# One GELU for both blocks in group 0, w1's last rows loaded whole, powers on GpSimd and a new order in a state-space and MLP kernel

## The chip, the cores and the metric

The kernel runs on one core of a Trainium2 chip. The core has a matrix engine (TensorE, PE in the profile), an engine for element-wise work (VectorE, DVE), one for activation functions (ScalarE, ACT), a general one (GpSimd, POOL), a queue engine that mostly starts transfers (SyncE, SP), and 16 DMA engines. Each engine takes its own instructions strictly in order, and they wait for one another through semaphores. The metric is the device time of one execution in microseconds; smaller is better.

## The reference

The input x has 2048 rows (a sequence) of 448 channels, in bf16. A layer norm gives xn. One path is a diagonal complex state-space layer: with dt = exp(log_dt) and a complex Lambda, each state decays by exp(dt * Lambda) from row to row, takes B_bar @ xn and is read by C. The other path is an MLP over a second layer norm: 448 to 1792 channels, GELU, back to 448. Its silu gates the first path.

```python
def _A_ref(x, ...):
    Lam, Bmat, Cmat = Lambda_re + 1j * Lambda_im, B_re + 1j * B_im, C_re + 1j * C_im
    dt = jnp.exp(log_dt)
    Lam_bar = jnp.exp(dt * Lam)
    B_bar = ((Lam_bar - 1.0) / Lam)[:, None] * Bmat
    Bu = jnp.einsum("bld,pd->blp", x + 0j, B_bar)
    for t in range(L):
        h = Lam_bar[None, :] * h + Bu[:, t, :]
    y = 2.0 * jnp.einsum("blp,dp->bld", hseq, Cmat).real + x * Dskip
def _B_ref(x, w1, b1, w2, b2):
    h = _gelu(_layernorm(x) @ w1 + b1)
    return h @ w2 + b2
xn = _layernorm(x)
return x + _A_ref(xn, ...) * _silu(_B_ref(xn, ...))
```

## The kernel before, in words

**Tiling.** The 2048 rows form four groups g of 512. A group has two blocks b; a block has 128 partitions, each with two neighbouring rows (par 0 and 1). The MLP's hidden width is 14 tiles of 128, worked in seven pairs.

**Stages of a group.** `ln_stats`, `ln_scale` and `ln_apply` give xn and xn2 (the norm of the norm, folded into one scaling). `ln_scale` takes an inverse square root, on POOL with the operation power (L480) or on DVE by Newton steps (L478 to L488). DMA transposes give xnT and xn2T. `mm1_run` multiplies xn2T by w1 (PE at L801) and applies GELU out of PSUM (ACT at L805) into gT. `mm2` multiplies by w2 (PE at L828), adds b2 (DVE at L831), and the silu follows. `bu` (L729) is the input product of the state-space layer, `ssm` (L744 to L775) its scan on DVE, `m0` (L697, L712) products of CQ and Bn that are needed once, and `ym` (L871 to L877) the output product. The final multiply and add stand at L885 to L891, and the add runs on DVE or POOL. `combine` (L658 to L661) scales rows of B and C into Bn, CQ and CZ: one scaled copy into `tmp` (ACT or DVE) and one fused multiply-add on DVE.

**mm1.** Each matmul uses 64 of the 128 partitions, so two run side by side on the halves of the array. A pair of tiles takes a first phase of 6 and a second of 8 matmuls, into two PSUM banks out of the list `MB`; `pairs` says which bank pair a tile pair takes. The 448 rows of w1 lie in four slots: 0 to 2 hold rows 0 to 383, and slot 3 holds rows 320 to 447. Its low half (rows 320 to 383) is a copy of the high half of slot 2, made by DVE or ACT at L352; its high half is loaded. w1 is loaded in four column chunks, each as a large piece (`w1_c`) and a small one (`w1r_c`).

**Group 0.** It starts while its data arrive. Block 0 is normalised first (`first_stats`, `first_apply`): ACT forms the inverse root as exp(-0.5 ln v) at L434/L435 for block 0 and L438/L439 for block 1. PE transposes the blocks at L460 instead of a DMA. mm1 of group 0 then has five pairs for block 0 alone, two pairs for both blocks, and five pairs for block 1 alone. A one-block pair has matmuls and GELUs of 256 columns, a two-block pair of 512. dt and the size of the pole are exponentials on ACT, at L533 and L541. After those ACT loads the GELU's table (L443), and it changes tables twice more near group 0 (L614 for silu, L618 for GELU).

**What sets the order.** A `Plan` records every task with what it reads and writes. `link` derives the dependencies, and `emit` issues the tasks in the fixed list `ORDER` and puts semaphore waits where they are needed. A task recorded with `either` has two engines to choose from, and the list `SECOND` names those that take the second. Thus each engine's queue, and the queues of transfers on SP and POOL, are a projection of this one list. SP's queue starts with x, w1, more of x, w2, then B and C, and then the transposes.

## Time and profile before

| what | value |
|---|---|
| median of 3 runs | 153.23 us (153.21 to 153.32) |
| profiled execution | span 151.8 us |
| PE busy | 147.1 us (97%) |
| DVE busy | 127.6 us (84%) |
| ACT busy | 99.0 us (65%) |
| POOL busy | 42.1 us (28%) |
| moved by DMA | 14.73 MB, mean 97 GB/s |

The span is the profiled execution from its first to its last event; the runs' times are those of whole executions and hold some work around it. An engine's share is its busy time over the span; register, branch and semaphore instructions are not counted. The page also cuts the span into 40 slices. A group line gives source line, engine, operation, tiles, shape and count, then busy time with the mean of one in ns, then the idle time just before and what ended it. A row of the timeline gives its start and length in us, and `x42` says that 42 like instructions stand in it. An issue line of the DMA view gives the size and the time from issue to landing.

### The profile page before, as it was taken

What the parts mean: (1) busy time and instruction counts of PE and PEld (TensorE: products, weight loads), DVE (VectorE), ACT (ScalarE), POOL (GpSimd) and SP (SyncE); (2) the same over time, 40 slices, a digit from 0 to 9 for tenths busy, and PEclk for the clock granted to TensorE, in tenths of its full rate; (3) what the DMA queues carried; (4) which work ended last, traced back from release to release, by engine and by line L of the source; (5) the groups of instructions that cost most, each with busy time, mean ns of one, the idle gap of its engine ahead of it and who ended that gap; (6) DMA issues with size and microseconds to landing.
All of it is one profiled execution on the core that took longest, in us unless ns stands there. A gap on an engine that the chain in (4) does not pass through costs nothing.

```text
span 151.8 us, 2974 instructions
## 1 busy us (share of the span) xinstructions
PE 147.1 (97%) x1127; PEld 86.6 (57%) x1127; DVE 127.6 (84%) x267; ACT 99.0 (65%) x183; POOL 42.1 (28%) x101
## 2 busy tenths in 40 slices
PE   7899999999999999999999999999999999999992
PEld 7785755454566577545444556764454666555551
DVE  2874999999978979999999996379968726999984
ACT  3888996988789559997898610463579834067400
POOL 5376827153020920010456006200072031000201
PEclk9999999999999999999999999999999999999999
DMA  4999999989997300700003032610331001100022
GB/s 116 262 305 390 266 202 138 219 152 133 165 261 180 65 0 0 138 0 4 0 0 63 4 60 45 154 60 4 60 101 23 0 4 57 64 0 0 4 84 98
DMA packets 31236, 14.73 MB, mean 97 GB/s; under 512 B 24752, under 2 KB 30774, under 8 KB 31222
## 3 DMA queue, kind: packets, MB, share of 16 engines
q1 hardware_dynamic: 30912, 14.26, 41.8%
q0 software_dynamic: 160, 0.23, 1.0%
q8 instruction: 9, 0.15, 0.4%
q10 hardware_dynamic: 150, 0.05, 0.1%
q14 instruction: 5, 0.04, 0.1%
HBM read 6.89 MB, written 1.84 MB: 57 GB/s over the span
## 4 chain that ended last, share of the span: by engine, by line
PE 80%; DVE 9%; DMA 4%; SPq 4%; issue 2%
PE psum L828 23%; PE psum L801 22%; PE psum L729 14%; PE psum L871 13%; DMA x_all<-in_A_x_dram 4%; PE psum L874 4%; SPq L84 4%; PE psum L712 3%; DVE xn_sb L499 2%; DVE lnst L399 1%; DVE s_w L628 1%; PE psum L877 1%; DVE o L831 1%; PE psum L697 1%; DVE tmp L891 1%
## 5 line engine op out<-in xcount | busy, mean ns | idle before, releaser
L801 PE MATMUL psum<-xn2T,w_sb 64*128 64x512 bf16 (+1 forms) x462 | 44.6, 345 | 0.3 <-ACT xn2T L417 0.2
L828 PE MATMUL psum<-w_sb,gT 128*128 128x448 bf16 x224 | 44.5, 353 | 0.2 <-DVE o L831 0.2
L805 ACT ACTIVATE gT<-psum,b1f 128x512 bf16<-128x512 f32 (+1 forms) x66 | 35.9, 625 | 10.4 <-PE psum L801 10.2
L801 PEld LDWEIGHTS psum<-xn2T,w_sb 64*128 64x128 bf16 x462 | 24.1, 109 | 19.8 <-ACT gT L805 2.3
L828 PEld LDWEIGHTS psum<-w_sb,gT 128*128 128x128 bf16 x224 | 21.5, 98 | 20.7 <-DVE o L831 0.6
L417 ACT ACTIVATE u_sb<-psum 128x512 bf16<-128x512 f32 (+2 forms) x22 | 10.5, 478 | 23.0 <-PE psum L729 22.7
L729 PE MATMUL psum<-xnT,BT 128*128 128x256 bf16 x196 | 24.0, 273 | 0.0
L729 PEld LDWEIGHTS psum<-xnT,BT 128*128 128x128 bf16 x196 | 18.9, 98 | 5.4 <-issue 1.1
L891 POOL TENSOR_TENSOR tmp<-t,x_all 128x448 bf16<-128x448 bf16 x5 | 5.2, 1032 | 33.1 <-DVE t L888 30.7
L753 DVE TENSOR_TENSOR_SCAN s_w<-dk,vs 128x774 f32<-128x774 f32 x8 | 14.0, 1760 | 0.1
L500 ACT ACTIVATE xn_sb<-x_all,lnw 128x448 bf16<-128x448 bf16 (+2 forms) x21 | 13.0, 662 | 1.2 <-DVE xn_sb L499 1.1
L417 ACT ACTIVATE vs<-s_w 64x256 bf16<-64x256 f32 (+2 forms) x16 | 10.9, 681 | 2.6 <-DVE s_w L753 1.5
L871 PE MATMUL psum<-CZ,h_sb 128*128 128x448 bf16 x56 | 11.9, 352 | 0.0
L871 PE MATMUL psum<-CQ,h_sb 128*128 128x448 bf16 (+2 forms) x54 | 10.5, 332 | 0.0
L399 DVE BATCH_NORM_STATS2 lnst<-x_all 128x6 f32<-128x448 bf16 x12 | 7.1, 617 | 3.4 <-DMA x_all<-in_A_x_dram 3.4
L831 DVE TENSOR_TENSOR o<-psum,b2bc 128x448 f32<-128x448 f32 x16 | 9.7, 614 | 0.2
L871 PEld LDWEIGHTS psum<-CZ,h_sb 128*128 128x128 bf16 x56 | 5.4, 98 | 4.7 <-DVE lnmv L405 0.4
L871 PEld LDWEIGHTS psum<-CQ,h_sb 128*128 128x128 bf16 x54 | 5.1, 98 | 4.0 <-DVE t L885 0.4
L874 PE MATMUL psum<-M,xnT 128*128 128x448 bf16 x32 | 7.4, 352 | 0.0
L480 POOL TENSOR_TENSOR lnw<-lnw,mhalf 128x8 f32<-128x8 f32 x3 | 7.2, 2404 | 0.3
L883 DVE TENSOR_TENSOR Cr<-psum,xd 128x448 f32<-128x448 f32 x7 | 4.3, 620 | 3.5 <-PE psum L877 3.4
L499 DVE TENSOR_SCALAR xn_sb<-x_all,lnw 128x448 bf16<-128x448 bf16 (+2 forms) x19 | 6.9, 396 | 0.0
(160 smaller groups left out, 189.1 us busy)
## 6 DMA issues: line engine op xcount, KB each, us to landing
out_dram<-tmp SPq DMA_DIRECT2D x7, 224.0 KB, 2.0
x_all<-in_A_x_dram SPq DMA_DIRECT2D x3, 448.0 KB, 4.0
w_sb<-in_B_w_dram SPq DMA_DIRECT2D x3, 448.0 KB, 8.4
w_sb<-in_B_w_dram SPq DMA_DIRECT2D x3, 384.0 KB, 4.8
vs<-in_A_C_re_dram SPq DMA_DIRECT2D x1, 392.0 KB, 11.6
Bn<-in_A_B_im_dram SPq DMA_DIRECT2D x1, 336.0 KB, 10.2
Bn<-in_A_B_re_dram SPq DMA_DIRECT2D x1, 336.0 KB, 10.5
vs<-in_A_C_im_dram SPq DMA_DIRECT2D x1, 336.0 KB, 10.8
```

The source lines that it names most:

```text
L399: dve([lambda e, b=b, par=par, q=q: e.bn_stats(lnst[:, q, :], x_all[:, 2 * g + b, par, :])], [f"x{2 * g + b}"] , [f"st{q}"], 0.62, prio)
L417: kb.either(("act", [lambda e, o=o, i=i: e.activation(o, i, ACT.Copy) for o, i in pairs]), ("dve", [lambda e, o=o, i=i: e.tensor_copy(o, i ...
L499: on = [("dve", [lambda e, o=o, i=i: e.tensor_scalar(o, i, rs, nb, op0=ALU.mult, op1=ALU.add) for o, i in parts], 0.4, 0.12), ("act", [lam ...
L500: ("act", [lambda e, o=o, i=i: e.activation(o, i, ACT.Identity, bias=nb, scale=rs) for o, i in parts], 0.75, 0.2)]
L729: fns = [lambda e, r=r, m=m, d=d: e.matmul(psum[:, 4, r * NK:(r + 1) * NK], BT[:, m, d, :], xnT[:, gx, d, :], start=(d == 0), stop=(d == 6 ...
L753: dve(lambda e, so=so, vi=vi: e.tensor_tensor_scan(so, dk[:].rearrange("p i c -> p (i c)"), vi, 0.0, ALU.mult, ALU.add), ["v", "vl", "dk", ...
L801: return lambda e: e.matmul(view(bk[k]), w1_sb[rows, d, fcol(2 * j + k)], rhs[rows, d, :, :], start=not second and n == 0, stop=second and ...
L805: act([lambda e, k=k: e.activation(gT[:, gb, 2 * j + k, :].rearrange("p (r c) -> p r c", r=2)[:, :, cols], view(bk[k]), ACT.Gelu_apprx_tan ...
L828: fns = [lambda e, fi=fi: e.matmul(psum[:, bk, 0:D], gT[:, gb, fi, q * 128:(q + 1) * 128], w2_sb[:, fi, :], start=(fi == 0), stop=(fi == N ...
L831: dve(lambda e: e.tensor_tensor(o2[:, fb, :], psum[:, bk, 0:D], b2bc[:], ALU.add), [f"ps{bk}", "b2bc"], [f"oo{fb}"], 0.62, prio - 76)
L871: fns = [lambda e, k=k: e.matmul(psum[:, bk, c0:c1], h_sb[:, hb, k, k0:k0 + 128], cm[:, k, c0:c1], start=(k == 0), stop=False) for k in ra ...
L874: fns += [lambda e, d=d: e.matmul(psum[:, bk, c0:c1], xnT[:, gx, d, xs], M0[:, d, c0:c1], start=False, stop=(d == 3)) for d in range(4)]
```

## The change

The change has five parts.

1. w1's slot 3 is loaded whole (128 rows of each chunk, from row 320 on), and the four copies at L352 are gone.
2. Block 1's inverse root is formed by one small DVE operation and a power on POOL, in place of Ln and Exp on ACT.
3. dt and the pole's size are formed by POOL as powers of e; a new tile `euler` holds e. The load of the GELU's table does not wait for them or for block 1's root.
4. mm1 of group 0 runs pairs 1, 2, 0 for block 0 without a GELU, the same pairs for block 1 in the same banks, then a GELU over both blocks for each of the three; pairs 3 to 6 run for both blocks at once.
5. `ORDER` and `SECOND` are new throughout. w2's first piece is issued ahead of the last w1 piece and of x for group 1, and C_im ahead of w2's last piece; both row broadcasts by POOL (b2 and Dskip) are issued together; the first product `m0` follows the first `bu` of group 0; five of the final adds go from DVE to POOL.

```diff
--- before.py
+++ after.py
@@ -160,27 +160,26 @@
 ORDER = [int(k) for k in """
-0 13 19 47 9 16 18 20 14 1 94 26 17 95 91 27 92 21 15 24 48 4 96 12 108 93 90 109 97 104 103 25 105 99 22 98 49 50 55 5 51 65 106 2 110 100 111 107 29
+17 9 16 20 14 0 91 92 19 25 18 88 4 44 15 13 1 21 89 93 87 106 45 90 46 5 107 2 96 102 24 27 101 26 3 22 108 48 100 23 12 103 29 104 30 47 28 94 52
...
 SECOND = [int(k) for k in """
-45 53 54 61 63 66 69 74 76 83 112 130 133 158 160 162 163 165 177 184 185 187 189 190 220 222 224 226 228 230 238 248 249 258 266 268 331 362 364 365
+42 50 51 54 59 69 72 73 74 75 76 81 83 84 98 105 110 119 144 151 152 185 209 211 213 217 219 223 225 229 235 237 247 251 257 325 334 339 341 343 351
...
@@ -223,6 +222,7 @@
 
         ident = SB("ident", [128, 128])
         mhalf = SB("mhalf", [128, 1, 1], F32)
+        euler = SB("euler", [128, 1], F32)
         dk = SB("dk", [128, 3, NK + 2], F32)
         iota = dk[:, 0, 0:NK]
         sgn = SB("sgn", [128, 4], F32)
@@ -324,6 +324,7 @@
             pool(lambda e: e.memset(M0[:, 3, :], 0.0), [], ["M0p"], 0.3, S0 + 1)
             pool(lambda e: e.memset(h_sb[:, :, :, 0:2], 0.0), [], ["hp0", "hp1"], 0.2, S0 + 1)
             pool(lambda e: e.memset(mhalf[:], -0.5), [], ["mhalf"], 0.1, S0 + 1)
+            pool(lambda e: e.memset(euler[:], math.e), [], ["euler"])
             pool(lambda e: e.memset(eps[:, 0:1], LN_EPS), [], ["eps"], 0.1, S0)
             pool(lambda e: e.memset(eps[:, 1:2], LN_EPS * LN_EPS), ["eps"], ["eps"], 0.1, S0)
 
@@ -345,11 +346,7 @@
             def ldw1(cs, prio):
                 a, w = CH[cs[0]][0] * 128, sum(CH[c][1] for c in cs) * 128
                 ld("sp", w1_sb[:, 0:3, a:a + w], dram_ap(B_w1, a, [[F, 128], [128 * F, 3], [1, w]]), [f"w1_{c}" for c in cs], 384 * w * 2, prio, dur=0.55)
-                ld("sp", w1_sb[64:128, 3, a:a + w], dram_ap(B_w1, 384 * F + a, [[F, 64], [1, w]]), [f"w1r_{c}" for c in cs], 64 * w * 2, prio)
-                for c in cs:
-                    a, w = CH[c][0] * 128, CH[c][1] * 128
-                    low, high = w1_sb[0:64, 3, a:a + w], w1_sb[64:128, 2, a:a + w]
-                    kb.either(("dve", lambda e, low=low, high=high: e.tensor_copy(low, high)), ("act", lambda e, low=low, high=high: e.activation(low, high, ACT.Copy)), [f"w1_{c}"], [f"w1c_{c}"])
+                ld("sp", w1_sb[:, 3, a:a + w], dram_ap(B_w1, 320 * F + a, [[F, 128], [1, w]]), [f"w1r_{c}" for c in cs], 128 * w * 2, prio)
 
             LW = ((0,), (1,), (2,), (3,))
 
@@ -434,13 +431,13 @@
                         kb.add("act", [lambda e, var=var, r1=r1: e.activation(r1, var, ACT.Ln, scale=1.0 + LN_EPS, bias=eps[:, 1:2]),
                                        lambda e, r1=r1: e.activation(r1, r1, ACT.Exp, scale=-0.5)], [f"mv0_{q}", "eps", "warm"], [f"r1{q}"], chain=True)
                     elif par == 1:
-                        vs2, rs2 = lnmv[:, 0, 1:4:2, 1], lnw[:, 0, 2, 1, 1:4:2]
-                        kb.add("act", [lambda e: e.activation(rs2, vs2, ACT.Ln, scale=1.0 + LN_EPS, bias=eps[:, 1:2]),
-                                       lambda e: e.activation(rs2, rs2, ACT.Exp, scale=-0.5)], ["mv0_1", "mv0_3", "eps", "warm"], ["r11", "r13"], chain=True)
+                        vs2, ws2, rs2 = lnmv[:, 0, 1:4:2, 1], lnw[:, 0, 1, 1, 1:4:2], lnw[:, 0, 2, 1, 1:4:2]
+                        small(lambda e: e.tensor_scalar(ws2, vs2, 1.0 + LN_EPS, LN_EPS * LN_EPS, op0=ALU.mult, op1=ALU.add), ["mv0_1", "mv0_3"], ["w11"])
+                        pool(lambda e: e.tensor_tensor(rs2, ws2, mhalf[:, 0, :].to_broadcast([128, 2]), ALU.pow), ["w11", "mhalf"], ["r11", "r13"])
 
             def gelu_table():
                 kb._sem("gelu0")
-                kb.add("act", lambda e: e.preload_act_table_set("gelu_apprx_tanh_and_others"), ["cr", "r10", "r12"] + ["r11", "r13"] * (not 0), ["Wg0"], sem="gelu0")
+                kb.add("act", lambda e: e.preload_act_table_set("gelu_apprx_tanh_and_others"), ["r10", "r12"], ["Wg0"], sem="gelu0")
 
             def first_apply(b):
 
@@ -530,7 +527,7 @@
                    + [lambda e, i=i: e.matmul(psum[64 * i:64 * i + 64, 7, 12:15], vrows[0:3, 448:512], ident[0:3, 0:3], start=True, stop=True) for i in range(2)],
                    ["vr0", "vr1", "vr2", "ident"], ["ps7"])
                 act(lambda e: e.activation(cw[:, 0:3, :], psum[:, 7, 0:16].rearrange("p (t v) -> p v t", v=4)[:, 0:3, :], ACT.Copy), ["ps7"], ["cp"])
-                act(lambda e: e.activation(col(DT), col(LDT), ACT.Exp), ["cp", "warm"], ["cdt"], 0.2, 3 * PINNED - 4, "exp")
+                pool(lambda e: e.tensor_tensor(col(DT), euler[:].to_broadcast([128, 4]), col(LDT), ALU.pow), ["cp", "euler"], ["cdt"])
                 small(lambda e: e.tensor_scalar(col(F2), col(LIM), 1.0 / TWO_PI, None, op0=ALU.mult), ["cp"], ["f2"])
                 YA, YB, YC, YD = (ang[:, k, :, :, :] for k in range(4))
                 A2 = 2 * PINNED
@@ -538,7 +535,7 @@
                 small(lambda e: e.tensor_scalar(col(F2), ang[:, 0, 0, 0, :], 2.0, None, op0=ALU.mult), ["f1"], ["f2"])
                 small(lambda e: e.tensor_scalar(ang[:, 0, 0, 1, :], ang[:, 0, 0, 0, :], 512.0, None, op0=ALU.mult), ["f1"], ["f3"])
                 small(lambda e: e.tensor_tensor(col(A1), col(DT), col(LRE), ALU.mult), ["cdt", "cp"], ["ca"])
-                act(lambda e: e.activation(col(R1), col(A1), ACT.Exp), ["ca"], ["cr"], 0.2, 3 * PINNED - 1, "exp")
+                pool(lambda e: e.tensor_tensor(col(R1), euler[:].to_broadcast([128, 4]), col(A1), ALU.pow), ["ca", "euler"], ["cr"])
                 wrap = [(lambda e: e.tensor_scalar(YB, YA, ROUND, None, op0=ALU.add)),
                         (lambda e: e.tensor_scalar(YB, YB, ROUND, None, op0=ALU.subtract)),
                         (lambda e: e.tensor_tensor(YA, YA, YB, ALU.subtract))]
@@ -794,23 +791,24 @@
                 def phase(j, second):
 
                     c = chunk[2 * j]
-                    bk = MB[pairs[j - js[0]]]
+                    bk = MB[pairs[js.index(j)]]
 
                     def one(k, n, h):
                         rows, d = slice(64 * h, 64 * h + 64), (0, 1, 2 + h, 3 - h)[n]
                         return lambda e: e.matmul(view(bk[k]), w1_sb[rows, d, fcol(2 * j + k)], rhs[rows, d, :, :], start=not second and n == 0, stop=second and n == 3)
                     pe([one(h if not second else 1 - h, n, h) for n in range(4 if second else 3) for h in (0, 1)],
-                       xk2 + [f"w1_{c}", f"w1r_{c}"] + ([f"w1c_{c}"] if second else []), [f"ps{bk[0]}", f"ps{bk[1]}"], split=True)
-                    if second:
-                        act([lambda e, k=k: e.activation(gT[:, gb, 2 * j + k, :].rearrange("p (r c) -> p r c", r=2)[:, :, cols], view(bk[k]), ACT.Gelu_apprx_tanh,
+                       xk2 + [f"w1_{c}", f"w1r_{c}"], [f"ps{bk[0]}", f"ps{bk[1]}"], split=True)
+                    if second and not (g == 0 and b == 0):
+                        gc = slice(0, 256) if g == 0 else cols
+                        act([lambda e, k=k: e.activation(gT[:, gb, 2 * j + k, :].rearrange("p (r c) -> p r c", r=2)[:, :, gc], psum[:, bk[k], :].rearrange("p (r c) -> p r c", r=2)[:, :, gc], ACT.Gelu_apprx_tanh,
                                                          bias=b1f[:, 2 * j + k:2 * j + k + 1]) for k in range(2)],
                             ["b1f"] + [f"ps{k}" for k in bk] + [f"Wg{wg(g)}"],
-                            [f"gT{gb}_{2 * j + k}_{q}" for k in range(2) for q in ((0, 1) if b is None else (b,))])
-
-                for j in js:
+                            [f"gT{gb}_{2 * j + k}_{q}" for k in range(2) for q in (0, 1)])
+
+                for a, j in enumerate(js):
                     phase(j, False)
-                    if j > js[0]:
-                        phase(j - 1, True)
+                    if a:
+                        phase(js[a - 1], True)
                 phase(js[-1], True)
 
             def wg(g):
@@ -920,12 +918,10 @@
             dummies(3, ["st0"])
             first_apply(0)
             b1_columns()
-            N1, NP = 5, 3
-            PR = ((0, 1, 2, 0, 1), (2, 0), (1, 2, 0, 1, 2))
-            mm1_run(0, 0, range(5), PR[0])
+            mm1_run(0, 0, (1, 2, 0), (0, 1, 2))
             first_apply(1)
-            mm1_run(0, None, range(5, 7), PR[1])
-            mm1_run(0, 1, range(5), PR[2])
+            mm1_run(0, 1, (1, 2, 0), (0, 1, 2))
+            mm1_run(0, None, (3, 4, 5, 6), (3, 0, 1, 2))
             ln_scale(0, 2 * PINNED + 3, (1,))
             carry_table()
             for b in range(2):
```

2 lines of the change are left out of this document (1 added, 1 removed), and 31 rows, old and new, of the table ORDER.

## The prediction

> **What bounds the kernel now.** First I read the page's engine line, its clock line and the shares of the chain that ended last:
>
> ```profile
> span 151.8 us, 2974 instructions
> PE 147.1 (97%) x1127; PEld 86.6 (57%) x1127; DVE 127.6 (84%) x267; ACT 99.0 (65%) x183; POOL 42.1 (28%) x101
> PEclk9999999999999999999999999999999999999999
> PE 80%; DVE 9%; DMA 4%; SPq 4%; issue 2%
> ```
>
> TensorE is busy for 97% of the span and the granted clock is near full in every slice. The next view is the windows for PE alone (length, busy time with instructions, clock, DMA share, GB/s):
>
> ```profile
> 9.84:19.03 9.19, 9.06 (x128) 1.00 1.08 326
> 19.03:30.08 11.05, 10.87 (x58) 1.00 1.14 189
> 30.08:77.40 47.32, 47.32 (x371) 1.00 0.47 89
> 77.40:148.35 70.95, 70.95 (x465) 1.00 0.18 44
> 148.35:151.80 3.45, 0.56 (x7) 0.98 0.22 68
> ```
>
> From 30.08 to 148.35 us PE never waits: busy time equals window length. Work taken from other engines there gains nothing, while every wait that the new order makes is paid in full. Time can be gained only ahead of 30.08 (the start and group 0's MLP) or after 148.35 (3.45 us of tail). Ahead of 30.08 the DMA engines are full as well (shares of 1.08 and 1.14). The PE rows of that stretch, and of the next block of work (start, length, line, tiles, count):
>
> ```profile
> 6.85 2.50 PE L801 MATMUL psum<-xn2T,w_sb 64*128 64x256 bf16 x42 [0.19 <-ACT xn2T L417]
> 9.28 0.62 PE L460 MATMUL psum<-ident,xn_sb 128*128 128x128 bf16 x8
> 9.84 9.26 PE L801 MATMUL psum<-xn2T,w_sb 64*128 64x256 bf16 x126
> 30.08 10.11 PE L801 MATMUL psum<-xn2T,w_sb 64*128 64x512 bf16 x90
> 40.12 1.70 PE L729 MATMUL psum<-xnT,BT 128*128 128x256 bf16 x14
> 48.46 1.49 PE L712 MATMUL psum<-CQ,Bn 128*128 128x448 bf16 x7
> ```
>
> Durations are those of one execution with a span of 151.8. The median of the runs is 153.23, so 1.43 us lie around the span; I make the sum in the span and carry this over.
>
> **Fewer matmuls in group 0.** L801 goes from 140 small (64x256) and 28 wide ones to 84 small and 56 wide, for the same columns. A small one costs 2.50/42 = 0.0595 us, a wide one 10.11/90 = 0.1123. After: 84 x 0.0595 + 56 x 0.1123 = 5.00 + 6.29 = 11.29; before 2.50 + 9.26 = 11.76. That includes before's gaps on PE (9.06 busy of 9.19, and small matmuls waiting for banks), so the saving of 0.47 assumes that none comes back. Transposes stay at 0.62 (0.56 to the next start). With the start at 6.85 as before, mm1 of group 0 ends at 6.85 + 11.29 + 0.56 = 18.70, against 19.03; w1's first chunk leading with the 128-row piece may start it 0.2 earlier. I take 18.6, a gain of 0.4.
>
> **One GELU for both blocks.** The group, and its two shapes apart (count, busy, mean ns, idle before):
>
> ```profile
> L805 ACT ACTIVATE gT<-psum,b1f 128x512 bf16<-128x512 f32 (+1 forms) x66 | 35.9, 625 | 10.4 <-PE psum L801 10.2
> L805 ACT ACTIVATE gT<-psum,b1f 128x512 bf16<-128x512 f32 x46 | 28.3, 687 | 10.0 <-PE psum L801 9.9
> L805 ACT ACTIVATE gT<-psum,b1f 128x256 bf16<-128x256 f32 x20 | 7.8, 483 | 0.4 <-PE psum L801 0.3
> ```
>
> Twenty of 0.483 become ten of 0.687: 9.7 - 6.9 = 2.8 us less on ACT, which idled 10 us here for PE; on the path nothing. The price is that six banks stay full until block 1 has passed. With block 1 begun at 9.95 the first GELU starts after 20 small matmuls, at 11.1; the three pairs are read by 12.5, 13.9 and 15.2 (two of 0.69 each). PE is back at their banks after 42 small matmuls and 6, 20 and 34 wide ones: 13.1, 14.7 and 16.3. So no wait, with 0.6 us to spare at the least.
>
> **Copies of w1 and its longer load.** The copies' group, then the issues of the last piece of w2 (from a window at 9.0), of C_im and of the two transposes of xn2T, each with KB and us from issue to landing, and SP's row for the two:
>
> ```profile
> L352 DVE COPY w_sb<-w_sb 64x512 bf16<-64x512 bf16 x3 | 0.9, 291 | 1.1 <-DMA w_sb<-in_B_w_dram 1.0
> w_sb<-in_B_w_dram SPq DMA_DIRECT2D x1, 448.0 KB, 9.6
> vs<-in_A_C_im_dram SPq DMA_DIRECT2D x1, 336.0 KB, 10.8
> xn2T<-xn_sb SPq DMA_TRANSPOSE x1, 4.8
> xn2T<-xn_sb SPq DMA_TRANSPOSE x1, 5.1
> 21.67 3.21 SPq L83 DMA_TRANSPOSE xn2T<-xn_sb x2
> ```
>
> Four copies (about 1.1 us of DVE, off the path) go; 224 KB of loads come. The window's 326 KB per us prices them at 0.7 us of a full queue. The last piece of w2 (448.0 KB; issued at 9.0, so landed near 18.6) now stands behind this and behind 336.0 KB of C_im, 560 KB in all, or 1.7 us: it lands near 20.3. Where the queue runs at the later window's 189 KB per us the delay is 3.0 and the landing 21.6. mm2's first row needs it after 10 of 14 tiles, at 18.6 + 10 x 0.19 = 20.5. The wait is between 0 and 1.1; I take 0.1, since the bytes move mostly in the first window. mm2 then hands over at 18.6 + 0.1 + 11.05 = 29.75. The two transposes of group 1's xn2T (issued from 21.67 on, landed near 26.5 and 28.6) stand behind 0.7 more of loads: 29.3, just before. So group 1's mm1 starts at about 29.75 instead of 30.08: 0.3 gained.
>
> **Block 1's factors and both exponentials by power.** What ACT and DVE do for block 1, and what POOL's rows show of such work:
>
> ```profile
> 6.60 0.29 ACT L438 ACTIVATE lnw<-lnmv,eps 128x2 f32<-128x2 f32 x1
> 6.92 0.20 ACT L439 ACTIVATE lnw<-lnw 128x2 f32<-128x2 f32 x1
> 7.51 0.70 DVE L453 TENSOR_SCALAR xn_sb<-x_all,lnmv,lnw 128x448 bf16<-128x448 bf16 x2
> 5.42 0.26 POOL L540 TENSOR_TENSOR cw<-cw 128x4 f32<-128x4 f32 x1 [2.55 <-ACT cw L533]
> L480 POOL TENSOR_TENSOR lnw<-lnw,mhalf 128x8 f32<-128x8 f32 x3 | 7.2, 2404 | 0.3
> 9.30 1.90 POOL L480 TENSOR_TENSOR lnw<-lnw,mhalf 128x8 f32<-128x8 f32 x1
> ```
>
> No row has a power over 2 or 4 elements. One over 8 takes 1.90 here and 2.404 on the mean; an ordinary operation over 4 takes 0.26. Between these bounds I scale the mean by elements: 1.2 for four, 0.6 for two. In the rebuilt order POOL does the power for dt (from about 5.4 to 6.6), one multiply (0.26) and then the power for block 1: ready at 7.5, against 7.12 before. DVE's two applies then end at 8.2 to 8.7 and the transposes stand on PE after 28 small matmuls (6.85 + 1.67 = 8.5), with 14 more behind them as cover for the copies out of PSUM. So up to 0.2 us may be lost there; it lies within the 0.1 between 18.70 and my 18.6. At the cheap end nothing changes; at the dear end (1.90 each, POOL ready at 9.5) PE waits some 1.5. The exponential of the pole comes later on POOL and feeds only the tables, not the GELU's table load.
>
> The rule that speaks against this part is in the Trainium skill, "SBUF — State Buffer", section "Who interferes with whom": GpSimd's port belongs to a pair shared with VectorE, locked for a whole instruction, so that the other one blocks. By it a DVE copy or apply would be held until a power ends. The trace's rows under the 1.90 us power:
>
> ```profile
> 9.54 0.62 DVE L624 TENSOR_SCALAR s_w<-dk,cw 128x256 f32<-128x256 f32 x2
> 10.08 0.75 DVE L417 COPY xn2T<-psum 128x512 bf16<-128x512 bf16 x2
> 10.86 0.29 DVE L352 COPY w_sb<-w_sb 64x512 bf16<-64x512 bf16 x1
> ```
>
> Five DVE instructions ran inside 9.30 to 11.20, and the copy took 0.29, the mean of its group. I price no lock; by the rule the sum would be up to a power's 1.2 us longer.
>
> **The new order.** Its largest move: the first product of CQ and Bn (L712) goes from behind three bu to behind the first one. It would start at 29.75 + 98 x 0.1123 + 1.64 = 42.4, not at 48.46, and CQ's last factor must be ready then, not at 47.6:
>
> ```profile
> 46.96 0.68 DVE L661 SCALAR_TENSOR_TENSOR CQ<-Cr,cw,tmp 128x448 bf16<-128x448 bf16 x1
> 20.40:42.12 21.72, 21.07 (x52) 1.00 1.04 167
> L891 DVE TENSOR_TENSOR tmp<-t,x_all 128x448 bf16<-128x448 bf16 x10 | 3.8, 386 | 0.1
> L891 POOL TENSOR_TENSOR tmp<-t,x_all 128x448 bf16<-128x448 bf16 x5 | 5.2, 1032 | 33.1 <-DVE t L888 30.7
> ```
>
> DVE is 97% busy from 20.40 to 42.12 before. In the rebuilt order it has 52 instructions from group 1's xn2 applies through the last CQ (14 combinations, 12 scalings, 11 applies and products over a row, 4 bias adds, 11 small ones); before's window has as many, of the same kinds, in 21.07 us. Begun near 20.0 they end at 41.1 without a wait, and at 41.7 with the window's own 0.65 of waits. That leaves 0.7 us for later loads of B, the transposed C and ACT's scalings. So it just fits: I take 0, with 0 to 1.5 as the bounds. Five final adds more on POOL (1.03 for 0.39) free 1.9 us of DVE late in the kernel, under PE, and cost the last store at most a few tenths either way. The moved loads, POOL's two row broadcasts and the b and C parts of SP's queue have no other reader on PE before 40 us.
>
> **Sum:** start-up 0.4, wait for w2 -0.1, after that 0: 0.3 us less. 153.23 - 0.3 = 152.9.
>
> **Rivals.**
> (a) All of start-up's gain arrives and more: powers at the cheap end, a first matmul 0.2 earlier, all gaps gone, transposes early. 0.47 + 0.2 + 0.3 of gaps in 19.03:30.08 is about 0.9: 152.3. The full DMA windows speak against it.
> (b) The change of loads eats it: mm1 ends early, but w2's last piece lands at 20.9 or the transposes at 30.0. Gain 0: 153.2. For it: DMA shares above 1 up to 30.08.
> (c) The other side: CQ's chain on DVE is late for the product at 42.4. Any wait is paid in full: from 0.3 us on the gain is gone, from 0.6 on the kernel is slower. At a lateness of 1.1 the time is 153.23 - 0.3 + 1.1 = 154.0. For it: DVE's 97%. Against it: C_im is loaded earlier and the group's statistics are moved behind.
> (d) Powers at the dear end, or the lock: PE stands 1.5 us at block 1's transposes, with 0.3 saved later: 154.4. The 1.90 row for the same unit speaks for it, the undisturbed DVE rows against.
>
> **Chances.** The forecast 0.36, (a) 0.10, (b) 0.16, (c) 0.24, (d) 0.14. A change below 0.2% (0.3 us) can't be told from none in this kernel. Faster: 0.32 of the forecast's and (a), 0.42. Same: 0.04 of the forecast's, 0.14 of (b)'s and 0.02 of (c)'s, 0.20. Slower: 0.02 of (b)'s, 0.22 of (c)'s and (d), 0.38. The forecast's own range is 152.6 to 153.1; the whole runs from (a) to just under (d), 152.2 to 154.2.
>
> **What would show it.** PE's L801 rows ending near 18.6 and the next group's starting at 29.6 to 29.9; ten wide GELUs without a PE wait before them; no PE idle of over 0.1 us at the first product of CQ. It is wrong if PE idles between block 0 and block 1 (d), at mm2's tenth tile or at group 1's start (b), or at CQ's first product (c); if PE idles nowhere before its last product and the tail has grown, POOL's final adds were mis-sized.

## The result

The changed kernel takes 161.50 us (median of 4 runs, 160.55 to 163.18) against 153.22 us before (153.21 to 153.32, 4 runs). It is about 8 us slower: a ratio of 1.0518, with a 95% interval of 1.047 to 1.0566. The ratios, here and below, leave out slow runs, here the longest, and are not those of the medians (they differ by up to a per cent, in experiment 6); the two longest runs here (162.23 and 163.18) had a mean granted clock of 0.989 and the others 1.0. The profiled execution is one of 160.77 us with a span of 158.7 and a clock of 1.0.

First the page's engine line, clock line and chain of the changed kernel:

```profile
span 158.7 us, 2912 instructions
PE 150.6 (95%) x1099; PEld 84.8 (53%) x1099; DVE 135.7 (86%) x282; ACT 88.4 (56%) x154; POOL 50.2 (32%) x107
PEclk9999999999999999999999999999999999999999
PE 64%; DVE 17%; ACT 9%; POOL 3%; DMA 3%; issue 2%; SPq 1%; DVEq 0%; ACTq 0%
```

PE has 28 matmuls fewer and is busy 3.5 us longer. The chain gives PE 64% where it gave 80%, but the windows show that PE is still nearly always busy (the same columns as in the prediction):

```profile
9.41:20.13 10.72, 10.32 (x114) 1.00 1.07 335
20.13:30.83 10.70, 10.70 (x58) 1.00 0.85 149
30.83:43.06 12.23, 11.84 (x99) 1.00 0.92 151
81.88:154.74 72.86, 71.49 (x461) 1.00 0.12 32
154.74:158.70 3.96, 0.00 (x0) 1.00 0.34 116
```

Busy time hides most of the loss, because the same work has become longer. The rows of PE's timeline that answer to those of before, and then, from before, its mm1 of another whole group:

```profile
7.20 1.72 PE L798 MATMUL psum<-xn2T,w_sb 64*128 64x256 bf16 x28 [0.47 <-DMA w_sb<-in_B_w_dram]
9.41 10.79 PE L798 MATMUL psum<-xn2T,w_sb 64*128 64x256 bf16 x112
20.13 10.77 PE L826 MATMUL psum<-w_sb,gT 128*128 128x448 bf16 x56
30.83 12.30 PE L798 MATMUL psum<-xn2T,w_sb 64*128 64x512 bf16 x98
44.91 1.50 PE L709 MATMUL psum<-CQ,Bn 128*128 128x448 bf16 x7
69.73 12.21 PE L798 MATMUL psum<-xn2T,w_sb 64*128 64x512 bf16 x98
96.25 1.31 PE L869 MATMUL psum<-CQ,h_sb 128*128 128x448 bf16 x6 [0.80 <-DVE t L883]
106.04 1.50 PE L869 MATMUL psum<-CZ,h_sb 128*128 128x448 bf16 x7 [0.30 <-DVE Cr L881]
```

```profile
105.66 10.85 PE L801 MATMUL psum<-xn2T,w_sb 64*128 64x512 bf16 x98
148.66 0.25 PE L877 MATMUL psum<-CQ,h_sb 128*128 128x192 bf16 x1
```

The same 98 matmuls of mm1 take 12.21 us in the changed kernel and 10.85 before. The chain of waits breaks this row into pieces, and the view of waits names what the weight loads (PEld) of L798 stood for (us in total, times, longest). First the chain of the changed kernel, then its weight loads' waits, then those of before:

```profile
69.80 0.77 PE psum L798 x6
70.62 1.71 PE psum L798 x14
72.37 1.05 PE psum L798 x8
```

```profile
PEld psum L798 <- PE psum L798: 10.6, 21, 0.6
```

```profile
PEld psum L801 <- PE psum L801: 0.7, 2, 0.3
```

The pieces are the phases: 6 is a first phase, 14 a second phase with the next pair's first phase, 8 a second phase. In the new list a pair's second phase (8 matmuls) often stands directly behind its own first phase (6), and there PE waits for its own last matmul to end: 21 times, against 2 before. The program itself asks for this wait. `emit` leaves out a wait of one PE task for another unless one of the two is marked `split`, and the phases of mm1 are the tasks so marked (with one product of `m0`):

```python
if t.eng == d.eng == "pe" and not (t.split or d.split):
    continue
...
eng.wait_ge(self.sems[sem], val)
```

This group has five such places, which makes (12.21 - 10.85) / 5 = 0.27 us each.

The parts of the difference in the two spans (158.7 - 151.8 = 6.9): the steps of mm1's matmuls, each from its start to the next start on PE, add up to 48.57 us against 44.30, so 4.3 more, which is the gaps less what the fewer matmuls save; mm1 starts at 7.20 instead of 6.85 (0.35); PE waits for DVE at two output products (0.80 and 0.30) and at the first CQ product (about 0.15); and the tail after PE's last matmul (before: 148.66 + 0.25 = 148.91 to 151.8) grows from 2.89 to 3.96 (1.07). Together 7.0, which is 6.9 within the rounding.

### The profile page after: what moved, and what is told of

Same layout as the page of the kernel before. It is cut to its first block, busy times and chain, and to the rows that moved or that the text cites. A ratio compares the mean times of both kernels' runs of the same rounds, so it can differ in the third digit from the quotient of the medians.

```text
span 158.7 us, 2912 instructions
## 1 busy us (share of the span) xinstructions
PE 150.6 (95%) x1099; PEld 84.8 (53%) x1099; DVE 135.7 (86%) x282; ACT 88.4 (56%) x154; POOL 50.2 (32%) x107
## 4 chain that ended last, share of the span: by engine, by line
PE 64%; DVE 17%; ACT 9%; POOL 3%; DMA 3%; issue 2%; SPq 1%; DVEq 0%; ACTq 0%
PE psum L798 21%; PE psum L826 17%; PE psum L726 11%; PE psum L869 9%; PE psum L872 3%; DMA w_sb<-in_B_w_dram 3%; PE psum L709 3%; DVE s_w L750 2%; DVE CQ L658 2%; DVE t L883 2%; ACT WT L637 2%; DVE tmp L656 2%; ACT xn_sb L497 2%; ACT tmp L655 1%; DVE xd L846 1%
## 5 line engine op out<-in xcount | busy, mean ns | idle before, releaser
L798 PE MATMUL psum<-xn2T,w_sb 64*128 64x512 bf16 (+1 forms) x434 | 47.6, 358 | 1.9 <-DMA w_sb<-in_B_w_dram 0.5
L803 ACT ACTIVATE gT<-psum,b1f 128x512 bf16<-128x512 f32 x56 | 34.7, 688 | 11.8 <-PE psum L798 11.5
L798 PEld LDWEIGHTS psum<-xn2T,w_sb 64*128 64x128 bf16 x434 | 21.8, 109 | 26.5 <-PE psum L798 10.6
L889 POOL TENSOR_TENSOR tmp<-t,x_all 128x448 bf16<-128x448 bf16 x10 | 11.2, 1127 | 41.9 <-DVE t L886 25.0
L750 DVE TENSOR_TENSOR_SCAN s_w<-dk,vs 128x774 f32<-128x774 f32 x8 | 15.2, 1924 | 0.0
L497 ACT ACTIVATE xn_sb<-x_all,lnw 128x448 bf16<-128x448 bf16 (+2 forms) x17 | 10.6, 658 | 0.3 <-DVE xn_sb L496 0.3
L414 ACT ACTIVATE vs<-s_w 128x1536 bf16<-128x1536 f32 (+2 forms) x6 | 5.6, 947 | 7.8 <-DVE s_w L750 7.8
L845 POOL TENSOR_TENSOR xd<-xn_sb,dbc 128x448 bf16<-128x448 bf16 x5 | 5.9, 1172 | 9.4 <-DVE Cr L881 9.4
L831 ACT ACTIVATE g_sb<-o 128x448 bf16<-128x448 f32 x8 | 4.2, 565 | 6.5 <-DVE o L829 6.4
L834 DVE SCALAR_TENSOR_TENSOR g_sb<-th,o 128x448 bf16<-128x448 f32 x8 | 6.4, 804 | 1.4 <-ACT th L833 1.4
```

Of the source, the lines that this page charges most:

```text
L414: kb.either(("act", [lambda e, o=o, i=i: e.activation(o, i, ACT.Copy) for o, i in pairs]), ("dve", [lambda e, o=o, i=i: e.tensor_copy(o, i ...
L497: ("act", [lambda e, o=o, i=i: e.activation(o, i, ACT.Identity, bias=nb, scale=rs) for o, i in parts], 0.75, 0.2)]
L750: dve(lambda e, so=so, vi=vi: e.tensor_tensor_scan(so, dk[:].rearrange("p i c -> p (i c)"), vi, 0.0, ALU.mult, ALU.add), ["v", "vl", "dk", ...
L798: return lambda e: e.matmul(view(bk[k]), w1_sb[rows, d, fcol(2 * j + k)], rhs[rows, d, :, :], start=not second and n == 0, stop=second and ...
L803: act([lambda e, k=k: e.activation(gT[:, gb, 2 * j + k, :].rearrange("p (r c) -> p r c", r=2)[:, :, gc], psum[:, bk[k], :].rearrange("p (r ...
L889: add = lambda e: e.tensor_tensor(o_sb[:, ob, par * D + c0:par * D + c1], t3[:, fb, c0:c1], res, ALU.add)
```

## The experiments

A list of more than 600 task numbers says nothing to a reader, so the diffs of the order are given by phase: `F3` is the first phase of the third pair pass, `S3` its second phase. Groups 1 to 3 have passes 0 to 6; group 0 has ten in the changed kernel. The other tasks stay in place, and each GELU follows its phases unless told otherwise. For before and after, the lists are:

```
before g1: F0 F2 S0 F1 S2 S1 F3 F5 S3 S5 F4 F6 S4 S6
before g2: F0 F2 S0 F1 S2 S1 F3 F5 S3 F4 S5 S4 F6 S6
before g3: F0 F1 S0 S1 F2 F3 S2 F4 S3 S4 F5 F6 S5 S6
after  g0: F1 F0 S1 S0 F2 S2 F3 S3 F4 S4 F5 S5 F6 S6 F7 F8 S7 S8 F9 S9
after  g1: F0 F2 S2 S0 F1 S1 F5 S5 F3 S3 F4 S4 F6 S6
after  g2: F0 S0 F1 S1 F2 S2 F3 F4 S3 S4 F5 S5 F6 S6
after  g3: F0 S0 F1 S1 F3 F2 S2 F4 S3 S4 F5 S5 F6 S6
```

Counted in the full lists, the places at which `S` stands right behind the `F` of its own pass on PE are 21 in the changed kernel and 2 in the kernel before (both in its group 0): as many as the waits in the two traces.

The theory: phases put back to back cost PE 0.23 us each, and wide work on POOL (operations of 448 columns) holds DVE. Besides the five final adds, the new choice of engines gives POOL two more products xd and one sum, so it has 16 such operations instead of 8 and, as before, one add of 256 columns. The rivals: one of the four other parts costs the time (the loads, the powers, the shared GELU), or DVE is late by itself.

**1. The changed kernel with phases interleaved throughout** (group 0 likewise, by its own numbers).

```diff
-g2: F0 S0 F1 S1 F2 S2 F3 F4 S3 S4 F5 S5 F6 S6
+g1, g2, g3: F0 F1 S0 F2 S1 F3 S2 F4 S3 F5 S4 F6 S5 S6
```

> The changed kernel with one edit in its order: in every group the first phase of the next pair of tiles stands again between the two phases of a pair (and the GELUs follow in that order), as in the kernel before; everything else keeps its place on its engine. Theory A (the order put both phases of a pair back to back, and PE waits 0.23 us for its own first phase each time, 22 times): the 22 gaps fall to at most 4, PE's gaps inside mm1 from 4.9 to under 0.7 us, and the time falls by 3 to 4.3 us from 161.5, to 157.2 to 158.5. Theory B (DVE is the bound in the later groups, held up by POOL): the gaps go but come back as PE waiting for DVE at the output products; the time stays above 159.5.

Measured: 165.06 us, 1.0771 of before (1.071 to 1.0833), slower still, where 157.2 to 158.5 was expected. The gaps are gone from PE's list, but other waits came, of which these are among the longest (line waited for: us, times, longest; lines are 6 higher here):

```profile
PE psum L732 <- ACT gT L809: 2.5, 1, 2.5
PE psum L804 <- DVE M L708: 1.5, 1, 1.5
PE psum L804 <- ACT gT L809: 1.3, 2, 0.9
PE psum L875 <- DVE t L889: 1.0, 1, 1.0
```

Here more pairs are open at once and share the same banks; PE then waits for GELUs, and the longest wait is bu's for a bank whose GELU stands on ACT behind a scaling that itself waits for DVE. So this run does not price the gaps: the rest of the new list does not fit the interleaved phases.

**2. The changed kernel without the wide POOL work.** Ten final adds go back to DVE, and so do five products xd and one sum.

```diff
 SECOND
-421 425 433 476 484 488 590 594 598 608
+238 353 354 496 497 601
```

> The changed kernel with its wide element-wise work on POOL (ten final adds of 448 columns, five products of xn with Dskip, one sum) given to DVE, same places in the order. Theory B (a wide POOL operation holds DVE up by 0.5 to 0.85 us, 9.4 us in all, against 2.6 before): DVE's instructions go back to their usual lengths (excess under 1.5 us) although DVE has sixteen instructions more, the two waits of PE for DVE's results (0.80 and 0.30 us) shrink, the tail is a us shorter, and the time falls by 1.5 to 2.5 us, to 159.0 to 160.0, with less spread between runs. Theory A alone: the 22 gaps stay, and DVE's longer list costs: 161.5 or more.

Measured: 159.07 us, 1.0406 (1.0342 to 1.0469): 2.4 us faster than the changed kernel by the medians, 1.8 by the profiled executions (159.00 against 160.77). One part of the expectation failed: the tail is 3.7 us, not a us shorter than 3.96. DVE has 16 instructions more than in the changed kernel and is busy 3.6 us less; its page's engine line, and two of its groups by form:

```profile
PE 150.3 (96%) x1099; PEld 85.2 (54%) x1099; DVE 132.1 (84%) x298; ACT 88.4 (56%) x154; POOL 31.5 (20%) x91
```

```profile
L840 DVE SCALAR_TENSOR_TENSOR g_sb<-th,o 128x448 bf16<-128x448 f32 x8 | 4.9, 618 | 2.5 <-ACT th L839 2.5
L852 DVE TENSOR_TENSOR xd<-xn_sb,dbc 128x448 bf16<-128x448 bf16 x8 | 3.2, 408 | 0.0
```

In the changed kernel the same two groups are longer, and its timeline shows where (POOL and DVE rows of one stretch):

```profile
L834 DVE SCALAR_TENSOR_TENSOR g_sb<-th,o 128x448 bf16<-128x448 f32 x8 | 6.4, 804 | 1.4 <-ACT th L833 1.4
L846 DVE TENSOR_TENSOR xd<-xn_sb,dbc 128x448 bf16<-128x448 bf16 x3 | 2.4, 837 | 0.0
```

```profile
93.19 1.11 POOL L889 TENSOR_TENSOR tmp<-t,x_all 128x448 bf16<-128x448 bf16 x1 [7.28 <-DVE t L883]
93.33 1.45 DVE L834 SCALAR_TENSOR_TENSOR g_sb<-th,o 128x448 bf16<-128x448 f32 x1
94.71 0.95 DVE L770 TENSOR_TENSOR h_sb<-pa,pb 128x1536 bf16<-128x1536 bf16 x1
95.58 0.61 DVE L883 SCALAR_TENSOR_TENSOR t<-psum,g_sb 128x448 bf16<-128x448 f32 x1
```

The operation at L834 usually takes 0.62 and takes 1.45 beside a POOL add that runs to 94.30. What stands behind it on DVE ends at 96.19, and the output product at 96.25 is the one that waited 0.80 us. That product runs without a wait in this experiment, and so does the one that waited 0.30.

**3. Both edits together.**

```diff
+the order of experiment 1
+SECOND of experiment 2
```

> Both edits at once: phases interleaved and no wide work on POOL. If A and B are the whole loss and independent, 161.5 - 4 - 2 = 155.5, within 0.7; what is left above 153.2 is then the start (0.35 us later) and single waits for DVE. If one hides the other, the time is that of the better single edit.

Measured: 161.78 us, 1.0559 (1.0509 to 1.0608): 3.3 us less than with the interleaving alone. That is far above the expected 155.5, because the waits for banks stay (1.7 us at bu, for one). The price of wide POOL work is there in both orders.

**4. The kernel before, with its phases put back to back**, all else as it was, in two forms.

```diff
-g1: F0 F2 S0 F1 S2 S1 F3 F5 S3 S5 F4 F6 S4 S6
+first form,  g1 to g3: F0 S0 F1 S1 F2 S2 F3 S3 F4 S4 F5 S5 F6 S6
+second form, g1, g2:   F0 S0 F2 S2 F1 S1 F3 S3 F5 S5 F4 S4 F6 S6
+second form, g3:       F0 S0 F1 S1 F2 S2 F3 S3 F4 S4 F5 S5 F6 S6
```

> The kernel before with one edit in its order: in groups 1 to 3 the two phases of a pair stand back to back, as in most of the changed kernel. Theory A: 19 gaps of 0.23 us on an engine that is never idle, 4.4 us: 157.2 to 157.8. If the gap is an effect of something else in the changed kernel (DVE, banks), the time stays within 1 us of 153.2.

> The kernel before, groups 1 to 3 with each pair's first phase moved to stand right ahead of its second, the second phases and the GELUs in their old order (e4 had them in another, which added waits for banks). Theory A: up to 20 gaps of 0.23 us and nothing else, 4.6 us, all of it in the time: 157.4 to 158.2.

The first form took 161.49 us, 1.0557 (1.0502 to 1.0612). Beside the gaps it had four waits for banks that cost 0.92 to 0.97 us each, because the GELUs stayed in the order of before, which was not the order of the second phases any more; so the second form keeps the two in step. It took 157.75 us (157.67 to 157.91), 1.0223 (1.0124 to 1.0323), 4.4 us more than before. Its view of waits, and its timeline's row of mm1 of group 1:

```profile
PEld psum L806 <- PE psum L806: 11.0, 21, 0.6
```

```profile
30.01 11.41 PE L806 MATMUL psum<-xn2T,w_sb 64*128 64x512 bf16 x90
```

21 waits against 2 is 19 more, and 4.35 / 19 = 0.23 us each. The row of 90 matmuls took 10.11 before and holds six of the places now: 1.30 / 6 = 0.22. Nothing but the order of the phases differs, so the price of a gap is shown here by itself. PE's busy time is 150.0 us here, against 147.1 for the same matmuls before, so busy time does not show these waits.

**5. Experiment 2 with twelve of the gaps taken out by six exchanges.**

```diff
-g0: ... F3 S3 F4 S4 F5 S5 F6 S6 ...
+g0: ... F3 F4 S3 S4 F5 F6 S5 S6 ...
-g1: ... F1 S1 F5 S5 ...
+g1: ... F1 F5 S1 S5 ...
-g2: F0 S0 F1 S1 ... F5 S5 F6 S6
+g2: F0 F1 S0 S1 ... F5 F6 S5 S6
-g3: ... F5 S5 F6 S6
+g3: ... F5 F6 S5 S6
```

> The run without wide work on POOL (e2), with the second phase of a pair and the first phase of the next one exchanged at six places on PE, where the next pair's banks are long free; the order of the GELUs and all other engines stay. Theory A (each back-to-back pair costs PE 0.23 us, and e1 was slower only because its plain order by number made PE wait for banks behind ACT's other work): twelve of 22 gaps go, 2.8 us, 159.1 - 2.8 = 156.3, within 0.6. Rival: the gaps are cover that PE needs anyhow for banks or for DVE; then a wait for ACT or DVE takes their place and the time stays above 158.3.

Measured: 160.63 us, 1.0409 (1.0308 to 1.051), not faster than experiment 2, where 156.3 was expected. The gaps are down to nine, and its view of PE's waits has these; below them the first row of mm1 in its timeline:

```profile
PE psum L804 <- DVE M L708: 1.1, 1, 1.1
PE psum L732 <- ACT gT L809: 0.5, 1, 0.5
PE psum L804 <- ACT gT L809: 0.4, 1, 0.4
```

```profile
7.29 3.15 PE L804 MATMUL psum<-xn2T,w_sb 64*128 64x256 bf16 x28 [0.55 <-DMA w_sb<-in_B_w_dram]
```

Exchanges at the end of a group make the next users of the banks (bu among them) wait for GELUs, as in experiment 1; the wait for DVE at L708 was there in experiment 2 (0.6) and is longer; and one output product waits 0.6 for DVE. These waits are 2.0 us more than in experiment 2, against 2.8 from twelve gaps. Besides, the first 28 matmuls took 3.15 us in this execution, where they take 1.72 in the changed kernel: an execution with a slow start. That is no effect of the exchanges, all of which stand behind these matmuls, and experiment 1's profile has a slow start as well.

**6. The four other parts with the order of before.** The code of the changed kernel, with the tasks and choices of engine of before as far as the tasks are the same.

```diff
-after g0: F1 F0 S1 S0 F2 S2 F3 S3 F4 S4 F5 S5 F6 S6 F7 F8 S7 S8 F9 S9
+      g0: F0 F1 S0 S1 F2 S2 F3 F4 S3 F5 S4 S5 F6 F7 S6 F8 S7 F9 S8 S9
-ORDER and SECOND of after
+ORDER and SECOND of before, for all other tasks
```

> All four parts of the change (w1's last rows whole, powers on POOL for block 1 and both exponentials, one GELU over both blocks for three pairs, w1's copies gone) in the order and with the engine choices of the kernel before; only group 0's mm1 and the new small operations are placed anew. Theory C (the loss is in the new order; the parts alone save the 0.3 us that the prediction's sum gave, group 0's MLP handing over 0.3 to 0.6 earlier): 152.6 to 153.2. Rival D (the parts themselves cost, by the longer load or the powers at block 1): 153.8 or more, with PE waiting at block 1's transposes, at w2 or at group 1's start.

Measured: 156.99 us (155.35 to 158.71), 1.0138 (1.0025 to 1.0251). mm1 ends where the prediction had it, and then PE stands. Timeline, and windows of PE around that place:

```profile
21.14 9.12 PE L832 MATMUL psum<-w_sb,gT 128*128 128x448 bf16 x39 [2.50 <-ACT gT L809]
```

```profile
18.64:21.14 2.50, 0.00 (x1) 0.97 1.03 236
21.14:24.50 3.36, 3.36 (x10) 0.52 1.58 148
24.50:28.00 3.50, 3.50 (x20) 1.00 0.83 194
```

The wait is a fault of this mixed list: the row with which mm2 begins is one piece, and so it waits for the last GELU of group 0, which stands on ACT behind one of three scalings for group 1 (L503). It costs twice, because the granted clock is 0.52 for the 3.36 us that follow. So this run, expected at 152.6 to 153.2, says nothing on the parts, and experiment 8 mends it.

**7. The kernel before, with about as much wide POOL work as the changed one**: 19 operations instead of 9, the add of 256 columns counted; the changed kernel has 17.

```diff
 SECOND
-249 364 365 612
+432 444 495 601 605 619
```

> The kernel before with the changed kernel's share of wide work on POOL: ten final adds, four products with Dskip and one sum more or less exchanged, 19 instead of 9 such operations on POOL, same places in the order. Theory B (a wide POOL operation holds DVE): DVE's excess over its usual lengths rises from 2.6 to 6 us or more, the slack of some 0.4 us at the last state products is used up, and the time rises by 1 to 3 us. If DVE isn't held, DVE has 4 us less to do and the time stays within 0.5 of 153.2.

Measured: 154.17 us (9 of 10 runs from 154.06 to 154.38) against 153.38, 1.0019 (0.9972 to 1.0065). The interval holds 1; in the trace, one new wait of PE (0.73 us, for DVE) stands against a span longer by 0.7:

```profile
142.60 1.29 PE L877 MATMUL psum<-CQ,h_sb 128*128 128x448 bf16 x6 [0.73 <-DVE h_sb L781]
```

The medians differ by 0.8 us, which is less than the 1 to 3 of the theory and more than the 0.5 of its rival. So the hold on DVE costs what DVE's slack doesn't cover: 0.8 at most in the order of before, 1.8 to 2.4 in the new one (experiment 2). That DVE has less slack there is inferred from these two prices.

**8. Experiment 6 mended.**

```diff
-ACT: ... one scaling of group 1 (L503), last GELUs, two scalings
+ACT: ... last GELUs, three scalings
-mm2 of group 0, first row: one piece
+mm2 of group 0, first row: three pieces, as in after
```

> As e6 (the four parts in the order of the kernel before), with group 0's hand-over fitted to the wide GELUs: the last GELU ahead of ACT's three normalisations, and mm2 beginning with the row that is cut into three pieces, so that it needs the last tiles only 2.3 us after its start. In e6 mm1 of group 0 ended near 18.5 us as the prediction's sum has it, and then PE stood 2.66 us for that last GELU. Theory C: without that wait mm2 starts at 18.5 to 18.7, group 1's mm1 at 29.4 to 29.8 against 30.08, and the time is 0.3 to 0.7 us under the kernel before: 152.6 to 153.0. Rival D (w2's last piece or the transposes hold it): at or above 153.2.

Measured: 153.44 us (12 runs, 152.80 to 154.80) against 153.49 (23 runs, 153.09 to 154.82): 0.9999 (0.9965 to 1.0032). Its span was 151.1:

```profile
9.22 9.52 PE L804 MATMUL psum<-xn2T,w_sb 64*128 64x256 bf16 x112
18.67 10.77 PE L832 MATMUL psum<-w_sb,gT 128*128 128x448 bf16 x56
29.37 10.11 PE L804 MATMUL psum<-xn2T,w_sb 64*128 64x512 bf16 x90
```

With all four parts and an order that fits, nothing is lost: the whole of the 8 us comes with the new lists, the order and the choice of engines. Its code is that of the changed kernel, so it prices the gaps a second time: mm1's steps add up to 43.77 us here and to 48.57 there, with 20 waits more, 0.24 each. mm1 of group 1 starts 0.71 us earlier than before (30.08); the spans agree with that (151.1 against 151.8), but the runs, expected at 152.6 to 153.0, can't tell it from none.

**9. The changed kernel with the large piece of w1's second chunk ahead of its 128-row piece**, as in before.

```diff
 ORDER
-... 2 96 102 24 27 101 26 3 22 ...
+... 2 96 102 24 101 26 27 3 22 ...
```

> The changed kernel with two loads exchanged on SP's queue: the large piece of w1's first chunk ahead of the 128-row piece, as before. Theory F: the first matmul then starts near 6.9 instead of 7.2, and PE's idle time just ahead of it falls from 0.47 to 0.2 us, so that executions in which the first 28 matmuls run at half speed (1.4 to 1.7 us) become rarer: 0.3 to 1.6 us off the median, 159.9 to 161.2. If the start has no part in it, 161.5.

Measured: 160.62 us (160.09 to 162.53), 1.0432 (1.0378 to 1.0487), 0.9 below the changed kernel's median; its lowest run is 0.5 below the lowest there, and the ranges overlap. mm1 starts without a wait for a load:

```profile
7.02 1.72 PE L804 MATMUL psum<-xn2T,w_sb 64*128 64x256 bf16 x28 [0.19 <-PE psum L606]
```

The start by itself is 0.18 us earlier. The rest of the difference between medians is within what runs of these kernels scatter; the profiled executions differ the other way (161.00 against 160.77), and both have 1.72 us for the first 28 matmuls, so a rarer slow start is not shown.

**10. Experiment 2 with the load of experiment 9 and three of experiment 5's exchanges, none at the end of a group.**

```diff
+SECOND of experiment 2, load order of experiment 9
-g0: ... F3 S3 F4 S4 F5 S5 F6 S6 ...
+g0: ... F3 F4 S3 S4 F5 F6 S5 S6 ...
-g2: F0 S0 F1 S1 ...
+g2: F0 F1 S0 S1 ...
```

> The changed kernel with three things mended: w1's large piece first, no wide work on POOL, and three exchanges of phases (twice in group 0, once in group 2) that leave the ends of the groups alone, since in e5 the exchanges there made the next user of the bank wait for a GELU. Expected from e2 (159.1): 0.35 for the start and 6 gaps of 0.23, less 0.5 where group 2 must wait for its first GELU all the same: 157.2 to 158.2. If it stays at 159, the gaps in this order are not a cost of their own.

Measured: 157.83 us (157.10 to 159.37), 1.0246 (1.0194 to 1.0299), within the 157.2 to 158.2 that were expected: by the medians 3.7 us of the 8.3 are back, 2.4 of them experiment 2's, by small edits in the same order. What is left, by the view of waits (of an execution of 159.37 with a slow start):

```profile
PE psum L804 <- DVE M L708: 1.0, 1, 1.0
PEld psum L804 <- PE psum L804: 7.9, 15, 0.6
```

Thirteen gaps more than before at 0.23 us are 3.0, the wait for DVE 1.0, the tail 0.8 (3.7 against 2.9), and the fewer matmuls give back 0.5: together about the 4.3 us that remain.

**11. Experiment 8 with block 0's second copy out of PSUM on DVE instead of ACT.**

```diff
 SECOND
+105
```

> e8 with block 0's second copy out of PSUM on DVE instead of ACT, so that both run at once: mm1 may start up to 0.4 us earlier (near 6.4 instead of 6.9), since w1's first pieces have landed by 6.3; block 1's statistics move 0.3 later on DVE and may take it back at the transposes. 0 to 0.4 us under e8.

Measured: 153.32 us (12 runs, 152.93 to 155.46), 0.9986 (0.9954 to 1.0017). mm1 starts at 6.85, not near 6.4. No version beats the kernel before by more than the runs can tell; the best that the parts give is no change.

## Why the prediction was wrong

It forecast 152.9 us with a range to 154.2, and the time is 161.5, outside of both. Steps in its own order:

- **What bounds the kernel** was right, and its warning too: "every wait that the new order makes is paid in full". The second form of experiment 4 puts 19 gaps into the order and pays for all of them, 4.35 us. But the evidence, "busy time equals window length", can't show a wait of this kind: it is counted as busy.
- **Fewer matmuls in group 0**: the step that failed is "the saving of 0.47 assumes that none comes back", and with it "after that 0" in the sum. The order of the phases in mm1 was not looked at, though the list holds it. Gaps came back in all groups: 21 waits of PE for its own matmuls, net 4.3 us. In group 0 the 112 matmuls after the transposes took 10.79 us, against 9.52 in experiment 8. With an order that fits (experiment 8) the arithmetic holds: hand-over to mm2 at 18.67 (predicted 18.6) and to group 1 at 29.37 (predicted 29.75).
- **One GELU for both blocks**: right. There is no wait of PE for these GELUs in the changed kernel.
- **Copies of w1 and its longer load**: "may start it 0.2 earlier" had the wrong sign. The first matmuls need both pieces of w1's second chunk, and with the 128-row piece in front both had landed only at 7.07; mm1 started 0.35 us later, after a wait of 0.47 for a load. With the large piece in front they had landed at 6.20 (experiment 9) and 6.28 (experiment 8), both with the longer second piece, and at 6.45 before, so it is the order of the two and not the longer load. w2's last piece landed at 19.92 (predicted 20.3), and mm2's window shows 10.70 us busy of 10.70: no wait.
- **The powers**: sizes right to some tenths, 1.04 and 1.59 us for four elements (predicted 1.2) and 0.70 for two (0.6). Block 1's transposes started at 8.86 without a wait for DVE. The powers' groups:

```profile
L530 POOL TENSOR_TENSOR cw<-euler,cw 128x4 f32<-128x4 f32 x1 | 1.0, 1044 | 0.0
L436 POOL TENSOR_TENSOR lnw<-lnw,mhalf 128x2 f32<-128x2 f32 x1 | 0.7, 700 | 0.0
```

- **"I price no lock"**: right for the powers, wrong for the kernel. The rows it was judged by lay under a power over 8 elements per partition, and two of the five are copies out of PSUM, a kind that no POOL operation holds in these traces. Wide POOL operations do hold DVE, and the new lists have more of them. Taking them off POOL gave 1.8 to 2.4 us (experiment 2). One place is in the tail, where a DVE row takes 1.22 beside a POOL add; the same operation takes 0.38 before (the timeline's row):

```profile
153.03 1.22 DVE L889 TENSOR_TENSOR tmp<-t,x_all 128x448 bf16<-128x448 bf16 x1
```

- **"Cost the last store at most a few tenths either way"**: the tail is 1.07 us longer. Only some 0.25 of this goes with the wide POOL work, for in experiment 2, without it, the tail is still 3.7 us. The rest comes with the new order, in which DVE's last work is later: a sum of x and Cr that began at 146.77 before, 2.1 us ahead of PE's end, begins at 153.12 in experiment 2, 0.4 ahead of it.
- **The new order**, the early CQ product: it waited about 0.15 us, inside the bounds of 0 to 1.5, but by luck. CQ's last factor was forecast for 41.1 to 41.7 and ended at 44.85:

```profile
44.16 0.69 DVE L658 SCALAR_TENSOR_TENSOR CQ<-Cr,cw,tmp 128x448 bf16<-128x448 bf16 x1 [0.44 <-ACT tmp L655]
```

  DVE had waited 1.8 us for mm2's first row and 1.1 for ACT, and POOL's products held it besides. The wait stayed small because PE was 2.5 us late as well: the product began at 44.91, not at 42.4. DVE's 52 instructions were as forecast and its 21.63 us of busy time nearly so; the waits were not.
- **The rivals**: none had the mechanism that decided. (c) was right that CQ's chain on DVE would be late, but PE's own lateness hid it; (d) named the lock, but at the powers.

What stays open: the profiled execution has 160.77 - 158.7 = 2.07 us outside its span, where executions of before have about 1.7 (153.32 with a span of 151.6, for one). In the new order it is 2.0 to 2.15 with the wide POOL work (experiments 1 and 9) and 1.7 to 1.8 without it (experiments 2, 3, 5 and 10), but experiment 7, with 19 such operations in the order of before, has 1.7. So 0.3 us of experiment 2's gain lies there, and no run gave a reason for it.

## What to carry to other kernels

Where an engine is busy throughout, read its own queue in the new order, instruction by instruction, for places at which it waits for itself: on TensorE, where the program waits for the matmuls just before, each wait costs 0.23 us with these tiles, and one independent phase in between hides it. An operation moved to GpSimd is not free for VectorE: look at what runs on VectorE in the same microsecond and whether that has slack. A list of this length is tuned as a whole; taking out single gaps moved the waits to the banks (experiments 1 and 5), while exchanges away from the ends of groups were part of what paid in experiment 10.

## What the runs showed of the hardware

- **A wait of TensorE for its own matmul** costs 0.22 to 0.24 us with these tiles (64 rows, 512 columns in most), by experiments 4 and 8. The group row gives a mean of 0.345 us for one matmul of L801 before, while its row of 98 (10.85 us) gives 0.11 us per matmul: they overlap, and a wait for the last one's end gives the overlap up. That this is the cause of the size is argued, not shown.
- **Wide GpSimd work holds some VectorE operations and not others.** Beside a POOL operation of 128x448, DVE operations with two operands in SBUF, copies, scalings and scans that began second took up to 0.85 us longer; the rows out of PSUM with one SBUF operand, such as L883 with 0.61 above, kept their length. Where DVE's operation had begun first, it kept its length and POOL's grew: beside a scan that began at 132.03 and took its usual 1.77, a POOL add from 132.07 on took 2.56 us instead of 1.03 (experiment 7). Summed over the kernel, DVE's rows exceed their usual lengths by 9.4 us in the changed kernel, by 2.6 before, by 5.3 in experiment 7 and by 1.0 in experiment 2. The Trainium skill, "SBUF — State Buffer", section "Who interferes with whom", says that GpSimd's ports are VectorE's second pair, that whichever of the two issues first holds the pair for its whole instruction, and that a VectorE instruction with at most one SBUF input outside the two-port modes does not contend. The wide operations agree with that; the powers over 2 to 8 elements do not, since DVE rows beside them had their usual length: a sum of two SBUF tiles (L752) that began under a power of 2.26 us took 0.96 (experiment 7), where it takes 0.95 elsewhere.
- **The clock after an idle stretch.** After 2.50 us without a matmul the granted clock was 0.52 for 3.36 us (experiment 6). But after 2.54 us without one it stayed at 1.00 in experiment 1; its row of PE and the window behind it:

```profile
45.97 1.69 PE L732 MATMUL psum<-xnT,BT 128*128 128x256 bf16 x14 [2.54 <-ACT gT L809]
45.97:52.00 6.03, 6.03 (x44) 1.00 0.70 148
```

  In some executions the first matmuls ran slow too: 2.87 us for 28 in experiment 10, where the granted clock was 0.50 from 8 to 10 us, and 3.15 in experiment 5, against 1.72 in the changed kernel. The idle time just ahead does not decide: it was 0.28 and 0.55 us in these two, and 0.47 in the changed kernel. The Trainium skill, "TensorE: Matmul & The Clock Gate", section "What's actually happening", puts the slow clock after an idle window of about 3.4 us and the return after a busy one as long, and calls the window free-running. The 3.36 us agree with the return; in experiment 6 an idle time shorter than the window was enough. What decides between experiments 1 and 6 is not shown.
